# Decode attention on one core: the rows of the two output stores laid out for eight DMA engines instead of sixteen

## The chip, the core and the metric

The kernel runs on one core of one Trainium2 chip. The metric is the device time of the program in microseconds (us). The kernel before the change took 184.66 us, the median of three runs (184.62 to 184.82).

A core has the engines TensorE (PE; its weight loads are PEld), VectorE (DVE), ScalarE (ACT), GpSimd (POOL) and SyncE (SP). SP does not compute here: it issues DMAs and waits. ScalarE issues some DMAs too. Either queue's DMAs are carried out by the core's 16 DMA engines. SBUF is the on-chip memory of 128 partitions, PSUM is where TensorE writes its sums.

## The reference

One step of decoding with a sliding window: 32 sequences, one query token each, 32 query heads over 8 key/value heads, a window of 512 positions of a cache of 2048, heads of 128 elements, bf16.

```python
W = min(4096, max(256, Sk // 4))                     # 512
q = (x @ wq).reshape(B, Sq, Hq, Dh)                  # 32 x 32 heads x 128
k = jnp.repeat(k_cache[:, :, Sk - W:, :], rep, axis=1)
v = jnp.repeat(v_cache[:, :, Sk - W:, :], rep, axis=1)
scores = jnp.einsum("bhqd,bhkd->bhqk", q, k) * (Dh ** -0.5)
p = softmax(scores, axis=-1)
o = jnp.einsum("bhqk,bhkd->bhqd", p, v)
return o.reshape(B, Sq, Hq * Dh) @ wo                # 32 x 1 x 512
```

## The kernel before

**Tiles and rounds.** The 32 sequences are worked on in eight rounds q of four sequences. For a round, one 4 MB load brings the keys (K_sb, two buffers) and one or two loads the values (V_sb, two buffers), with the 128 partitions holding 4 sequences x 8 heads x 4 quarters of the window. The orders of the work on TensorE, VectorE and ScalarE are written out by hand in three lists (PE_OPS, DVE_OPS, ACT_OPS, lines 19 to 33), SP's order of loads in a fourth (LOADS, line 35). Each entry is a letter and a round; semaphores between them come from the function `needs`.

**One round.** VectorE transposes the keys (T, line 499). TensorE makes the scores (S), VectorE their maxima (M), ScalarE the exponentials (X), VectorE divides by the sums (N). TensorE moves the probabilities to the partitions of the values (E), ScalarE gathers them (G), VectorE and ScalarE spread them with a mask (B), and TensorE multiplies with the values (P, line 391). VectorE and ScalarE copy the result out of PSUM (C), and TensorE folds it so that the 128 elements of a head lie where the last product needs them: the fold F (line 403) for 120 of the 128 elements, the fold H (line 412) for the other eight.

**The columns of the sums.** The result of F stands in PSUM and ScalarE copies it to `o_sel` (op D, `folded`, line 569); H's result goes to `o_ext` (op U, `folded_ext`, line 574). `o_sel` is 128 partitions x 30 x 32 columns and `o_ext` 64 x 8 x 32; the last index is the sequence. Round q writes the four neighbouring columns 4q to 4q+3.

**The last product.** When the last round's D and U are done, TensorE multiplies with wo (lines 429 and 443): the 32 columns of `o_sel[:, i, :]` are the weights, so column m becomes row m of the result. The four strips c of the output's 512 columns go to four groups of 32 partitions of `Y_ps`, with n = 2 (c % 2) + c // 2 as the strip of wo. wo itself comes in three pieces (line 275), issued after the last values. At the end VectorE copies partitions 0 to 63 of `Y_ps` to `out_sb[:, 0]` (line 532) and ScalarE partitions 64 to 127 to `out_sb[:, 1]` (line 590). So partition 32c+m of `out_sb`, for c of 0 and 1, holds half c of the output row of column m, 256 elements of bf16 or 512 bytes.

**The stores.** The function `store` (line 236) waits for both copies and issues one DMA for a half: SP stores half 0 as its last work, ScalarE half 1. Each takes 32 partitions to 32 rows of the output, 16 KB. Both add to the one semaphore `sem_out`, and after the end of the block SP waits for 32 there, 16 for each DMA (line 594). With that the program ends.

Of the kernel before, what the change touches and what calls it, by code (L numbers as in the profile page):

```python
# [48 lines left out]
def bass_standalone__sliding_block_cached__sampling_kernel(  # L49
# [45 lines left out]
    def needs(op):  # L95
        kind, q = op[0], op[1]
        spread = lambda q: [("B", q, h) for h in range(HKV)]
        picks = lambda q: [("C", q, r) for r in range(4)]
        d = []
        if kind == "T":  # L100
            d = [("S", q - 1, op[2])]
        elif kind == "S":
            d = [("T", q, op[2]), ("X", q - 1)]
        elif kind == "M":
            d = [("S", q, 1)]
        elif kind == "X":
            d = [("M", q), ("N", q - 1)]
        elif kind == "N":
            d = [("X", q), ("E", q - 1)]
        elif kind == "E":  # L110
            d = [("N", q), ("G", q - 1)] + [("U", p) for p in before(op, "H")]
        elif kind == "G":
            d = [("E", q)] + spread(q - NG)
        elif kind == "B":
            d = [("G", q), ("P", q - 2, 31)]
        elif kind == "P":
            d = spread(q) + picks(q - 1)
        elif kind == "C":
            d = [("P", q, 31), ("F", q - 2), ("H", q - 2)]
        elif kind == "F":  # L120
            d = picks(q) + ([("D", q - 1)] if q < NQ - 1 else [])
        elif kind == "D":
            d = [("F", q)]
        elif kind == "H":
            d = picks(q) + [("U", q - 1)] + [("G", p) for p in before(op, "E")]
        elif kind == "U":
            d = [("H", q)]
        return [ends[n] for n in d if n[1] >= 0]

    with ExitStack() as es:  # L130
# [15 lines left out]
        o_sel = sb("o_sel", [P, NI, B], BF16)  # L146
        o_ext = sb("o_ext", [64, NX, B], BF16)
# [28 lines left out]
        ps = es.enter_context(nc.psum_tensor("ps", [P, 8, 512], F32))  # L176
        S_ps, EP_ps, O_ps, F_ps, Y_ps = ps[:, 0], ps[:, 1], ps[:, 2:6], ps[:, 6], ps[:, 7]

        def folds(q):
            return (F_ps if q < NQ - 1 else S_ps)[:, 0:4 * NI]  # L180

# [11 lines left out]
        s = {n: sem(n) for n in names}  # L193
# [42 lines left out]
        def store(eng, c):  # L236
            eng.wait_ge(s["out_y"], 2)
            eng.dma_start(
                out.rearrange("b s (c n) -> c (b s) n", c=2)[c],
                out_sb[32 * c:32 * c + 32, :, :].rearrange("b e n -> b (e n)"),  # L240
            ).then_inc(sem_out, 16)

        @block.sync
        def _(sp):
            wait = Waits(sp)
            load_wq(1)
            wo_h = wo.rearrange("(h r) n -> h (r n)", r=DH)
            wo_r = wo_h[:, 0:4 * NI * D].rearrange("h (d m) -> h d m", d=4)
            for op in ops_of(" ".join(LOADS)):
                kind, q = op[0], op[1]  # L250
                if kind == "K":
                    if q >= 2:
                        wait([ends["T", q - 2, 1]])
                    sp.dma_start(K_sb[q % 2][:, :], rows(k_cache, q)).then_inc(sem_k[q % 2], 16)  # L254
                elif kind == "V":
                    if q == 1:
                        sp.wait_ge(s["pe_q"], 8)
                    r0, r1 = (4 * g for g in V_PIECES[q][op[2]:op[2] + 2])
                    if q >= 2:
                        wait([ends["P", q - 2, r1 // 4 - 1]])  # L260
                    sp.dma_start(  # L261
                        V_sb[q % 2][:, r0 * DH:r1 * DH], rows(v_cache, q, r0, r1)
                    ).then_inc(sem_v[q % 2][op[2]], 16)
                elif kind == "A":
                    wait([ends["Z", 0]])
                    h0, h1, k, p0 = HEADS[q]
                    n = (h1 - h0) // k
                    sp.dma_start(  # L268
                        wx_row[p0:p0 + 4 * n:1 if k == 4 else 4, :],
                        wo_h[h0:h1, 4 * NI * D:].rearrange("(k j) m -> j k m", k=k),  # L270
                    ).then_inc(sem_wx, 16)
                else:
                    wait([ends["T", NQ - 2, 1]])
                    i0, i1 = WOP[q]
                    sp.dma_start(  # L275
                        wo_sb[:, i0:i1, :].rearrange("p i n -> p (i n)"),
                        wo_r[:, :, i0 * D:i1 * D],
                    ).then_inc(sem_wo[q], 16)
            store(sp, 0)

        @block.gpsimd
# [43 lines left out]
        def _(pe):  # L325
# [73 lines left out]
            def fold(q):  # L399
                if q == 0:  # L400
                    pe.wait_ge(s["dve_c"], 7 + len(HEADS))
                for d in range(4):
                    ins = pe.matmul(  # L403
                        folds(q),
                        lhsT=F_sb[:, d].rearrange("p h d -> p (h d)"),
                        rhs=C_sb[:, q % 2, :, NI * d:NI * d + NI],
                        start=d == 0, stop=d == 3, tile_position=(0, 0),
                    )
                return ins
# [40 lines left out]
        def spread_args(q, h):  # L450
            return bd[:, q % 2, :, h, :], PTc[:, q % NG], mask[:, h:h + 1]

        def pick_args(q, r):
            pr = slice(32 * r, 32 * r + 32)
            return C_sb[pr, q % 2], O_ps[pr, :, r * DH:(r + 1) * DH]
# [78 lines left out]
        @block.scalar  # L534
        def _(act):
            wait = Waits(act)
            act.wait_ge(s["pool_j"], 1)
            act.activation(junk[:, 1:2], junk[:, 0:1], ACTF.Exp).then_inc(s["act_warm"], 1)
            for n in range(4):
                act.wait_ge(s["pe_q"], 2 * n + 2)  # L540
                act.activation(  # L541
                    Q_row[:, 1024 * n + 512:1024 * n + 1024], ps[:, 2 * n + 1], ACTF.Copy
                ).then_inc(s["act_q"], 1)
            act.wait_ge(s["dve_c"], 3)

            def exponential(q):
                return act.activation(  # L547
                    P_f32[:, :].rearrange("p (k r) -> p k r", k=KB),
                    S_ps.rearrange("p (r k) -> p k r", k=KB), ACTF.Exp,
                    bias=negmax[:, q:q + 1], scale=SCALE, accum_out=sums[:, q:q + 1],  # L550
                )

            def gather(q):
                return act.activation(  # L554
                    PTc[:, q % NG], EP_ps.rearrange("p (e r) -> p r e", e=REP), ACTF.Copy)

            def spread(q, h0, h1):
                for h in range(h0, h1):
                    o, i, m = spread_args(q, h)
                    ins = act.activation(o, i, ACTF.Copy, scale=m)  # L560
                return ins

            def pick(q, r0, r1):
                for r in range(r0, r1):
                    ins = act.activation(*pick_args(q, r), ACTF.Copy)  # L565
                return ins

            def folded(q):
                return act.activation(
                    o_sel[:, :, 4 * q:4 * q + 4],  # L570
                    folds(q).rearrange("p (b i) -> p i b", b=4), ACTF.Copy)

            def folded_ext(q):
                return act.activation(
                    o_ext[:, :, 4 * q:4 * q + 4],
                    EP_ps[0:64, 0:4 * NX].rearrange("p (b i) -> p i b", b=4), ACTF.Copy)

            def zero(_):
                act.wait_ge(s["pool_qbd"], 4 * NQ)
                return act.activation(  # L580
                    wx_row, junk[0:64, 0:1].to_broadcast([64, NX * D]), ACTF.Copy
                )

            run = {"X": exponential, "G": gather, "B": spread, "C": pick, "D": folded,
                   "U": folded_ext, "Z": zero}
            for op in orders["ACT"]:
                wait(needs(op))
                run[op[0]](*op[1:]).then_inc(op_sem["ACT", op[0]], 1)
            act.wait_ge(s["pe_Y"], 2)
            act.activation(out_sb[:, 1, :], Y_ps[64:128, 0:P], ACTF.Copy).then_inc(s["out_y"], 1)  # L590
            store(act, 1)

        regions.close()
# [29 lines left out]
```

## Time and profile before

| what | value |
|---|---|
| median of three runs | 184.66 us (184.62 to 184.82) |
| the profiled execution's own time | 184.67 us |
| its span, first to last instruction | 183.3 us |
| mean granted TensorE clock | 0.814 |
| TensorE busy | 121.8 us (66%) |
| VectorE busy | 106.6 us (58%) |
| ScalarE busy | 54.0 us (29%) |
| HBM read | 75.53 MB, 412 GB/s over the span |
| SP's DMA queue (q1) | 3553 packets, 75.52 MB |
| ScalarE's DMA queue (q10) | 112 packets, 0.05 MB |
| ScalarE copies to o_sel (line 569), eight | 271 ns median |
| ScalarE copies to o_ext (line 574), eight | 184 ns median |
| issue of the store, SP / ScalarE | 0.37 / 0.39 us, both begin at 181.56 us |
| store, from issue to landing, SP / ScalarE | 1.5 / 1.7 us |
| SP's last wait, for the stores | 0.9 us |

A line of the page's groups names the line of the program, the engine, the operation, the tiles as out<-in, the shape and the count; behind the bar stand the busy time, the mean of one instruction, and the idle time before these instructions with what ended it. The lower-case q behind an engine's name (SPq, ACTq) means its sequencer, which issues DMAs and waits. A busy share says little by itself: the stages have different limits, and the chain of waits tells which one sets the end.

### The profile page before, as it was taken

What the parts mean: (1) busy time and instruction counts of PE and PEld (TensorE: products, weight loads), DVE (VectorE), ACT (ScalarE), POOL (GpSimd) and SP (SyncE); (2) the same over time, 40 slices, a digit from 0 to 9 for tenths busy, and PEclk for the clock granted to TensorE, in tenths of its full rate; (3) what the DMA queues carried; (4) which work ended last, traced back from release to release, by engine and by line L of the source; (5) the groups of instructions that cost most, each with busy time, mean ns of one, the idle gap of its engine ahead of it and who ended that gap; (6) DMA issues with size and microseconds to landing.
All of it is one profiled execution on the core that took longest, in us unless ns stands there. A gap on an engine that the chain in (4) does not pass through costs nothing.

```text
span 183.3 us, 3872 instructions
## 1 busy us (share of the span) xinstructions
PE 121.8 (66%) x1676; PEld 59.3 (32%) x1676; DVE 106.6 (58%) x109; ACT 54.0 (29%) x101; POOL 17.1 (9%) x53
## 2 busy tenths in 40 slices
PE   0089204426798795449945995340799978999994
PEld 0034000011653452313521352000254533655573
DVE  0041999796469731973289326999825994703030
ACT  3000300010863357101651135001053693703040
POOL 7900050200100100002000200001000000000000
PEclk9999965555589999756995599655559999999999
DMA  6998999999998999999999999999999999999992
GB/s 226 411 501 358 458 458 447 393 415 458 458 426 372 458 454 426 401 429 458 427 415 415 452 427 418 415 451 451 415 415 411 433 418 433 422 435 408 429 380 72
DMA packets 3681, 75.80 MB, mean 414 GB/s; under 512 B 465, under 2 KB 561, under 8 KB 689
## 3 DMA queue, kind: packets, MB, share of 16 engines
q1 hardware_dynamic: 3553, 75.52, 96.6%
q8 instruction: 13, 0.21, 0.5%
q10 hardware_dynamic: 112, 0.05, 0.1%
q14 instruction: 3, 0.02, 0.0%
HBM read 75.53 MB, written 0.03 MB: 412 GB/s over the span
## 4 chain that ended last, share of the span: by engine, by line
DMA 76%; DVE 13%; SPq 4%; PE 3%; issue 3%; ACT 0%; DVEq 0%
DMA K_sb<-in_k_cache_dram 50%; DMA V_sb<-in_v_cache_dram 16%; DVE KT_sb L499 12%; DMA K_sb<-in_wo_dram 10%; PE ps L391 2%; SPq L268 2%; SPq L254 1%; SPq L261 1%; PE ps L429 1%; PE ps L361 1%; SPq L210 0%; DVE C_sb L524 0%; SPq L275 0%; DVE maxv L505 0%; ACT P_bf L590 0%
## 5 line engine op out<-in xcount | busy, mean ns | idle before, releaser
L499 DVE STREAM_TRANSPOSE KT_sb<-K_sb 128x4096 f32<-128x4096 f32 x16 | 70.6, 4434 | 11.2 <-DMA K_sb<-in_k_cache_dram 11.0
L391 PE MATMUL ps<-V_sb,bd 32*128 32x512 bf16 x1024 | 62.9, 397 | 3.8 <-DMA V_sb<-in_v_cache_dram 2.2
L361 PE MATMUL ps<-KT_sb,QBD 128*32 128x512 bf16 x256 | 26.1, 546 | 37.5 <-DVE KT_sb L499 26.9
L391 PEld LDWEIGHTS ps<-V_sb,bd 32*128 32x128 bf16 x1024 | 27.8, 97 | 36.2 <-issue 12.2
L361 PEld LDWEIGHTS ps<-KT_sb,QBD 128*32 128x32 bf16 x256 | 6.7, 115 | 53.8 <-DVE KT_sb L499 33.2
L547 ACT ACTIVATE P_f<-ps,negmax 128x512 f32<-128x512 f32 x8 | 5.5, 687 | 60.5 <-DVE negmax L507 60.5
L560 ACT ACTIVATE bd<-PTc,mask 128x512 bf16<-128x512 bf16 x31 | 20.1, 711 | 0.3
L565 ACT ACTIVATE C_sb<-ps 32x512 f32<-32x512 f32 x22 | 12.9, 588 | 23.4 <-PE ps L391 23.2
L318 POOL COPY QBD<-QT_sb 32x128 bf16<-32x128 bf16 x32 | 9.3, 289 | 106.4 <-PE ps L361 89.8
L519 DVE TENSOR_SCALAR bd<-PTc,mask 128x512 bf16<-128x512 bf16 x33 | 9.4, 349 | 14.0 <-ACT PTc L554 14.0
L524 DVE COPY C_sb<-ps 32x512 f32<-32x512 f32 x10 | 6.9, 693 | 13.9 <-PE ps L391 13.8
L403 PE MATMUL ps<-C_sb,F_sb 128*128 128x120 f32 x64 | 9.4, 291 | 6.8 <-ACT C_sb L565 6.5
L376 PE MATMUL ps<-P_bf,E_sb 128*128 128x128 bf16 x128 | 11.0, 254 | 0.8 <-DVE P_bf L513 0.8
L403 PEld LDWEIGHTS ps<-C_sb,F_sb 128*128 128x128 f32 x64 | 8.0, 195 | 9.6 <-ACT C_sb L565 8.3
L505 DVE TENSOR_REDUCE maxv<-ps 128x1 f32<-128x512 f32 x8 | 5.5, 687 | 9.4 <-PE ps L361 9.3
L376 PEld LDWEIGHTS ps<-P_bf,E_sb 128*128 128x128 bf16 x128 | 9.3, 115 | 4.9 <-DVE P_bf L513 2.8
L554 ACT ACTIVATE PTc<-ps 128x512 bf16<-128x512 f32 x8 | 4.8, 594 | 18.3 <-PE ps L376 18.2
L343 PE MATMUL ps<-V_sb,bd 128*128 128x512 bf16 x32 | 8.7, 441 | 0.8 <-DVE bd L461 0.8
L331 PE MATMUL ps<-bd 32*128 32x128 bf16 x4 | 0.6, 295 | 9.2 <-DMA bd<-in_x_dram 9.2
L461 DVE CAST bd<-ps 128x512 bf16<-128x512 f32 x1 | 0.7, 692 | 9.8 <-PE ps L331 9.8
L541 ACT ACTIVATE KT_sb<-ps 128x512 bf16<-128x512 f32 x4 | 2.1, 602 | 14.2 <-PE ps L343 14.2
L488 DVE CAST KT_sb<-ps 128x512 bf16<-128x512 f32 x4 | 2.5, 684 | 5.9 <-PE ps L343 5.9
(37 smaller groups left out, 43.9 us busy)
## 6 DMA issues: line engine op xcount, KB each, us to landing
K_sb<-in_k_cache_dram SPq DMA_DIRECT2D x8, 4096.0 KB, 25.2
V_sb<-in_v_cache_dram SPq DMA_DIRECT2D x5, 4096.0 KB, 29.6
V_sb<-in_v_cache_dram SPq DMA_DIRECT2D x4, 2048.0 KB, 20.6
V_sb<-in_wq_dram SPq DMA_DIRECT2D x2, 2048.0 KB, 9.8
K_sb<-in_wo_dram SPq DMA_DIRECT2D x1, 2560.0 KB, 17.2
V_sb<-in_v_cache_dram SPq DMA_DIRECT2D x1, 2304.0 KB, 14.2
V_sb<-in_v_cache_dram SPq DMA_DIRECT2D x1, 1792.0 KB, 14.8
K_sb<-in_wo_dram SPq DMA_DIRECT2D x1, 1024.0 KB, 19.1
```

Of the source, the lines that this page charges most:

```text
L318: pool.tensor_copy(QBD[pr, q % 2].rearrange("p (w t) (h c) -> p w t h c", w=2, h=HKV)[:, :, :, :, 4 * b:4 * b + 4], QT_sb[pr, q].rearrange ...
L343: ins = pe.matmul(ps[:, n], lhsT=xT_sb[:, kt, :], rhs=wq_sb[:, kt, n * 512:(n + 1) * 512], start=kt == 0, stop=kt == DKT - 1, tile_positio ...
L361: ins = pe.matmul(S_ps[32 * c:32 * c + 32, :], lhsT=QBD[:, q % 2, 2 * w + t, c0:c0 + 32], rhs=KT_sb[:, w, :, KB * h:KB * h + KB, t], start ...
L376: ins = pe.matmul(EP_ps[:, e * R:(e + 1) * R], lhsT=E_sb[:, k, e].rearrange("p m j -> p (m j)"), rhs=P_bf[:, k * R:(k + 1) * R], start=k = ...
L391: ins = pe.matmul(O_ps[:, b, :], lhsT=bd[pr, q % 2, 4 * g:4 * g + 4].rearrange("p r h e -> p (r h e)"), rhs=V_sb[q % 2][pr, 512 * g:512 * ...
L403: ins = pe.matmul(folds(q), lhsT=F_sb[:, d].rearrange("p h d -> p (h d)"), rhs=C_sb[:, q % 2, :, NI * d:NI * d + NI], start=d == 0, stop=d ...
L499: return dve.transpose(KT_sb[:, w].bitcast(F32).rearrange("p r c t -> p r (c t)"), K_sb[q % 2][:, :].bitcast(F32).rearrange("p (r w c) -> ...
L505: dve.tensor_reduce(maxv[:, q:q + 1], S_ps, AX.X, ALU.max).then_inc(s["dve_m"], 1)
L519: ins = dve.tensor_scalar(o, i, m, None, op0=ALU.mult)
L524: ins = dve.tensor_copy(*pick_args(q, r))
L560: ins = act.activation(o, i, ACTF.Copy, scale=m)
L565: ins = act.activation(*pick_args(q, r), ACTF.Copy)
```

## The change

The 32 columns of `o_sel` and `o_ext` are filled in another order, and the stores undo it. Round q holds the sequences 4q+i, i from 0 to 3. Before, sequence 4q+i had column 4q+i. After, with the sequence written as 8a+j (a from 0 to 3, j from 0 to 7), it has column 4j+a. For round q that is a = q // 2 and j = 4 (q % 2) + i, so the round writes the columns 16 (q % 2) + q // 2 + 4i: four columns with a step of four. Row m = 4j+a of the last product then belongs to sequence 8a+j, and the store's target is written as eight groups j of four rows a of 256 elements, in place of 32 rows of 256 elements. The source, 32 partitions of 512 bytes, stays as it is.

```diff
+        def columns(q):
+            first = 16 * (q % 2) + q // 2
+            return slice(first, first + 13, 4)
...
         def store(eng, c):
             eng.wait_ge(s["out_y"], 2)
             eng.dma_start(
-                out.rearrange("b s (c n) -> c (b s) n", c=2)[c],
+                out.rearrange("(a j) s (c n) -> c j (a s) n", a=4, c=2)[c],
                 out_sb[32 * c:32 * c + 32, :, :].rearrange("b e n -> b (e n)"),
             ).then_inc(sem_out, 16)
...
             def folded(q):
                 return act.activation(
-                    o_sel[:, :, 4 * q:4 * q + 4],
+                    o_sel[:, :, columns(q)],
                     folds(q).rearrange("p (b i) -> p i b", b=4), ACTF.Copy)
 
             def folded_ext(q):
                 return act.activation(
-                    o_ext[:, :, 4 * q:4 * q + 4],
+                    o_ext[:, :, columns(q)],
                     EP_ps[0:64, 0:4 * NX].rearrange("p (b i) -> p i b", b=4), ACTF.Copy)
```

The instructions on each engine and their number stay the same, and so does the number of DMAs.

## The prediction

> **What bounds the kernel now.** I read the chain of work that ended last, then the timeline of its end, then the groups that the diff touches, then the DMA queues and issues. The head of the chain:
>
> ```profile
> DMA 76%; DVE 13%; SPq 4%; PE 3%; issue 3%; ACT 0%; DVEq 0%
> ```
>
> Three quarters of the span are loads, and ScalarE, whose copies the diff re-addresses, has no share of the chain. The timeline of the end, from the last fold on:
>
> ```profile
> 177.65 0.27 ACT L569 ACTIVATE o_sel<-ps 128x120 bf16<-128x120 f32 x1 [1.15 <-PE ps L403]
> 177.88 0.19 ACT L574 ACTIVATE o_ext<-ps 64x32 bf16<-64x32 f32 x1
> 177.97 1.13 PEld L429 LDWEIGHTS ps<-K_sb,o_sel 128*32 128x32 bf16 x80 [0.24 <-ACT o_sel L569]
> ...
> 180.24 0.93 PE L429 MATMUL ps<-K_sb,o_sel 128*32 128x128 bf16 x40 [0.41 <-DMA K_sb<-in_wo_dram]
> ...
> 181.26 0.27 ACT L590 ACTIVATE P_bf<-ps 64x128 bf16<-64x128 f32 x1 [3.19 <-PE ps L429]
> 181.56 0.37 SPq L238 DMA_DIRECT2D out_dram<-P_bf  x1
> 181.56 0.39 ACTq L238 DMA_DIRECT2D out_dram<-P_bf  x1
> ```
>
> Columns: start, length in us, then the instruction, in brackets the idle time before it. TensorE, given the last o_sel at 177.9, stands idle 0.41 us for a piece of wo before 180.24: so much may o_sel come later at no cost. From 181.56 only the two stores are left, and SP's last wait is for them. The waits of SP, then the landing of the stores in the DMA view, then the stretch of the stores (length, five engines, clock, DMA share, GB/s):
>
> ```profile
> SPq L594 <- DMA out_dram<-P_bf: 0.9, 1, 0.9
> ```
>
> ```profile
> out_dram<-P_bf SPq DMA_DIRECT2D x1, 16.0 KB, 1.5
> out_dram<-P_bf ACTq DMA_DIRECT2D x1, 16.0 KB, 1.7
> ```
>
> ```profile
> 182.40:182.60 0.20, 0.00 (x0) 0.00 (x0) 0.00 (x0) 0.00 (x0) 0.00 (x0) 1.00 0.55 128
> 182.60:182.80 0.20, 0.00 (x0) 0.00 (x0) 0.00 (x0) 0.00 (x0) 0.00 (x0) 1.00 0.16 36
> 182.80:183.26 0.46, 0.00 (x0) 0.00 (x0) 0.00 (x0) 0.00 (x0) 0.00 (x0) 1.00 0.00 0
> ```
>
> The bytes move between 182.4 and 182.75; in the last 0.46 us nothing moves and SP still waits. The trace's single records of DMA packets and semaphore updates, which no view prints, divide the tail: issues until 181.932 (SP) and 181.956 (ACT); first packet of SP's store at 182.424, of ACT's at 182.509; 64 row packets of 512 B, most 27 to 40 ns, and 32 completion packets, 16 for each store, the last ending at 182.726; then 32 updates of the output's semaphore from 182.801 to 183.233, the first gap 31 ns and each of the other thirty 13 or 14 ns. The first update follows the first completion packet (182.479) by 0.32 us, the last follows the last (182.717) by 0.52. So the updates queue, for some 0.2 us, one in 13.3 ns. SP's wait ends at 183.249, the span at 183.27.
>
> The profiled execution took 184.67 us: the span and 1.40 us around it. The sum is made against 184.67; the median of the three runs is 184.66.
>
> **The change part by part.**
>
> *The ScalarE copies into o_sel and o_ext* (eight of each): same instructions, same elements, only that four columns lie 8 bytes apart. Rows: 271 and 184 ns, of 120 and 32 elements, so about 1 ns an element. No ScalarE row writes single bf16 elements; the near ones write runs of four or whole rows. Bounds: nothing, and a doubling of the part that goes by the element, +0.12 and +0.03 us. Even then the last pair delays TensorE by 0.15 us of the 0.41 it idles; the seven earlier pairs stand in an engine busy 29% and off the chain. I take 0. If the wo load landed 0.41 us earlier, the 0.15 would show.
>
> *TensorE* reads all 32 columns as before; only the order of the result's rows differs. 0. *The two result copies, 0.28 and 0.27 us*, are unchanged. 0.
>
> *Issue, engines.* Each store goes from 16 engines with two rows to 8 with four. The four loads of x on ScalarE's queue differ in this: 2, 6, 10 and 14 rows, as many completion packets. The timeline has
>
> ```profile
> 1.34 0.27 ACTq L204 DMA_DIRECT2D bd<-in_x_dram  x1
> ...
> 1.64 0.31 ACTq L204 DMA_DIRECT2D bd<-in_x_dram  x1
> ...
> 1.98 0.35 ACTq L204 DMA_DIRECT2D bd<-in_x_dram  x1
> ```
>
> for 6, 10 and 14 engines (271, 314, 351 ns): 10 ns an engine, and on to 371 ns for 16, where the stores have 373 and 392. Eight fewer engines: -0.08 us. Their semaphore got 36 updates where 2+6+10+14 is 32, so each DMA on fewer than 16 engines adds one for the missing count; these issues hold that cost.
>
> *Issue, dimensions.* The target becomes three-dimensional (8 by 4 by 256) against a source of 32 by 256. The K loads have such a shape against wq's plain rows:
>
> ```profile
> 0.74 0.42 SPq L210 DMA_DIRECT2D V_sb<-in_wq_dram  x1
> ...
> 43.49 0.54 SPq L254 DMA_DIRECT2D K_sb<-in_k_cache_dram  x1
> ```
>
> 0.54-0.42: +0.12 us. The two nearest in shape are loads of wo's remainder on five engines, 20 rows in groups of four (0.90 us) and five plain rows (0.73): +0.17. I take +0.12, since K's issue follows a wait on an idle queue, as the store's does. Ends: 0, and a whole issue as long as the 0.90. With the engines: 0.37-0.08+0.12 = 0.41, +0.04 us on each queue, the two side by side.
>
> *Issue to first packet.* 0.49 us with 16 engines (SP), 0.39 with two (x: issue ended at 1.302, packet at 1.695): 7 ns an engine at most, -0.06 for eight; ScalarE's 0.55 against 0.39 would be -0.09. I take 0, as one store's packets already waited on the other's, and keep -0.09.
>
> *Packets.* Both stores may land on the same eight engines: eight rows an engine instead of four. SP's first rows start over about 0.17 us from engine to engine (some 11 ns each), so the eighth starts at about 182.51; eight rows at 30 ns and two completions of 9 ns bring its end to 182.77, against 182.726: +0.04. Ends: -0.05 (ACT's store on other engines) and +0.30 (the stage of 0.30 us doubles). For the engines' choice, the Trainium skill (DMA: Bandwidth & Descriptors, Why a DMA increments its semaphore by 16 and not by 1) states that such a DMA takes the lowest-numbered ones and that the issuing sequencer writes the missing count at once; the 36 updates agree with the latter, and no view tells engines apart.
>
> *Updates.* 16 from engines instead of 32. Served one in 13.3 ns, 16 take 0.2 us; the first completion now comes after four rows (about 182.54), its update at 182.86, the sixteenth at 183.08 (one gap of 31, fourteen of 13.3). The last completion packet starts at 182.76 and its update is due 0.32 later, also 183.08 to 183.09. Against 183.233: -0.14 us, packets included. Ends: 0, if the gaps are those of rows being written, of which there are as many; -0.21, sixteen gaps saved whole.
>
> Sum: +0.04 (issue) +0 -0.14 (packets and updates) = -0.10 us: 184.57.
>
> **The rivals.**
>
> *The updates wait for rows, not for each other.* 64 rows in 0.43 us is 6.7 ns a row; the queue would then be as long as now. For: the rows of all engines go to one 32 KB region. Against: rows of many engines mix irregularly, and thirty equal gaps speak for a server of updates. Time: 184.67+0.04+0 = 184.71. The same skill page (Anatomy of one DMA, of GpSimd's path) lays most of a store's fixed time to the receipt from the target memory, which would give the same 184.71; the two completions of the x loads, with SBUF as target, were followed 0.34 us later by their updates, no less than the 0.32 here, so the trace does not bear it out.
>
> *Every per-engine cost halves and the shape costs nothing.* Issue -0.08, first packet -0.09, updates -0.21, packets 0: 184.29, just on the bound of a fall, and a little more if ScalarE's issue, now 392, falls with SP's to 0.29 (-0.10): 184.27. For: the rows of x carry all slopes. Against: K's dimension, the eight rows an engine.
>
> *Half the engines, double the transfer.* The skill page's section Rules for kernel authors says to keep a size that is a multiple of 16 outermost, so that all 16 engines are used. By rows: the packet stage of 0.30 us doubles and hides the shorter queue of updates: 184.67+0.30 = 184.97. Against: the starts are staggered and cover most.
>
> *The issue takes the long form, on the other side.* The nearest shape (20 rows, groups of four, five engines) took
>
> ```profile
> 157.37 0.90 SPq L268 DMA_DIRECT2D QT_sb<-in_wo_dram  x1
> ```
>
> Both stores at 0.90 instead of 0.37: +0.53, less the 0.14: 185.06. It makes the kernel slower by over 0.2% from an issue of 0.88 us on. Against: it stood in a row of issues beside running loads, and the plain issues behind it (0.73 to 0.63) were long too, with five and two engines.
>
> **How the numbers follow.** The forecast, 184.57, has 0.38 with its neighbours between 184.45 and 184.70; rows as the limit, 184.71, 0.13; all per-engine costs halved, about 184.27, 0.27; the doubled transfer, 184.97, 0.07; the long issue, 185.06 and more, 0.15. 0.2% is 0.37 us, about what a measurement of this kernel can tell from no change. Of the 0.27 I put 0.20 beyond 184.29: faster 0.20. Slower 0.15. The rest, 0.65, within. The range goes from 184.20 to 185.07: it leaves out some 0.05 below and half of the long issue above.
>
> **What would show it.** The issues of the stores at about 0.41 us instead of 0.37 and 0.39 (0.29: the shape is free; 0.90: the long form). The packets of ScalarE's queue fall from 112 to 104, of 32 completions 16 remaining. The updates: 16 of the engines and two single ones ahead, gaps of 13 ns (27 would say rows). Landing 1.6 at most for the later store instead of 1.7; SP's last wait shorter by about 0.1. The o_sel and o_ext copies at 271 and 184 ns. Wrong it would be, above all, if the loads before 180.9 took another time, which nothing in the change touches, or if the issue costs more than 0.9 us.

## The result and the profile after

The changed kernel takes 185.22 us (median of nine runs, 184.94 to 185.40) against 184.73 us for the kernel before beside it (nine runs, 184.62 to 184.96): slower by 0.28%, ratio 1.0028 with a 95% interval of 1.0020 to 1.0037. That is 0.49 us, and the time lies 0.15 us above the stated range.

The profiled execution of the changed kernel is its shortest run, 184.94 us, with a span of 183.62 us; its loads happened to end a little earlier, and the stores began at 181.44 us instead of 181.56. So spans are not compared here, but the tail from the first store's issue on: 1.71 us before, 2.18 us after, +0.48 us, close to the 0.49 us between the medians.

The timeline of the end of the changed kernel (start, length, instruction; lines of the program are four further on):

```profile
177.60 0.42 ACT L573 ACTIVATE o_sel<-ps 128x120 bf16<-128x120 f32 x1 [1.01 <-PE ps L407]
177.83 0.25 ACT L578 ACTIVATE o_ext<-ps 64x32 bf16<-64x32 f32 x1
178.07 1.12 PEld L433 LDWEIGHTS ps<-K_sb,o_sel 128*32 128x32 bf16 x80 [0.39 <-ACT o_sel L573]
...
180.13 0.92 PE L433 MATMUL ps<-K_sb,o_sel 128*32 128x128 bf16 x40 [0.20 <-DMA K_sb<-in_wo_dram]
...
181.14 0.27 ACT L594 ACTIVATE P_bf<-ps 64x128 bf16<-64x128 f32 x1 [3.06 <-PE ps L433]
181.44 0.78 SPq L242 DMA_DIRECT2D out_dram<-P_bf  x1
181.44 0.77 ACTq L242 DMA_DIRECT2D out_dram<-P_bf  x1
```

The issue of each store has doubled, 0.78 and 0.77 us instead of 0.37 and 0.39. The copy to o_sel takes 0.42 us instead of 0.27, and TensorE's idle time before the last piece of wo shrinks from 0.41 to 0.20 us (0.15 of that is the copy; the piece of wo also came a little earlier): the copy is slower, but still covered. The same tail in stretches (length, five engines, clock, DMA share, GB/s):

```profile
181.40:182.85 1.45, 0.00 (x0) 0.00 (x0) 0.00 (x0) 0.01 (x1) 0.00 (x0) 1.00 0.00 0
182.85:183.00 0.15, 0.00 (x0) 0.00 (x0) 0.00 (x0) 0.00 (x0) 0.00 (x0) 1.00 0.54 157
183.00:183.15 0.15, 0.00 (x0) 0.00 (x0) 0.00 (x0) 0.00 (x0) 0.00 (x0) 1.00 0.24 62
183.15:183.62 0.47, 0.00 (x0) 0.00 (x0) 0.00 (x0) 0.00 (x0) 0.00 (x0) 1.00 0.00 0
```

The first packet comes at 182.85, 1.41 us after the issue began; before, that took 0.87 us. Between first and last packet little has changed. The DMA queues and SP's waits say that the rows did go as intended:

```profile
q10 hardware_dynamic: 104, 0.05, 0.1%
```

```profile
SPq L598 <- DMA out_dram<-P_bf: 0.6, 1, 0.6
```

104 packets on ScalarE's queue instead of 112: eight completion packets fewer, so eight engines. SP's last wait became shorter, 0.6 us instead of 0.9, because it began later, and not because the stores landed sooner: a wait that shrinks is no gain by itself. Only half of that delay is the longer issue. Between the issue and the wait SP and ScalarE each have a DRAIN instruction at the end of their part of the block, which the timeline does not list; it too became longer (least, median and greatest length in ns), first before, then after:

```profile
L593 ACTq DRAIN  x1: 146/146/146, 182.0 to 182.0; - x1
L593 SPq DRAIN  x1: 116/116/116, 182.0 to 182.0; - x1
```

```profile
L597 ACTq DRAIN  x1: 492/492/492, 182.3 to 182.3; - x1
L597 SPq DRAIN  x1: 562/562/562, 182.3 to 182.3; - x1
```

Measured from the start of the issue, SP's wait begins 0.80 us later: 0.40 by the issue and 0.45 by SP's DRAIN, less some smaller gaps. So the issuing engines are held for some time after the issue has ended; whether the store's first packet waits for the same thing is not shown.

The single records of packets and semaphore updates divide the tail. "Issue" runs from the first issue's start to the later one's end, "to packet" on to the first packet, "packets" to the end of the last completion packet, "updates" to the last update of the output's semaphore, "end" to the end of the span. The other columns belong to the experiments below.

| us | before | after | e16x2 | inner | rows8 | one_plain | one_8x4 | packed |
|---|---|---|---|---|---|---|---|---|
| issue | 0.40 | 0.78 | 0.65 | 0.70 | 0.34 | 0.37 | 0.78 | 0.37 |
| to packet | 0.47 | 0.64 | 0.64 | 0.65 | 0.46 | 0.49 | 0.64 | 0.49 |
| packets | 0.30 | 0.27 | 0.49 | 0.50 | 0.18 | 0.23 | 0.17 | 0.30 |
| updates | 0.51 | 0.47 | 0.38 | 0.37 | 0.49 | 0.36 | 0.36 | 0.36 |
| end | 0.03 | 0.03 | 0.03 | 0.03 | 0.03 | 0.03 | 0.03 | 0.03 |
| sum | 1.71 | 2.18 | 2.20 | 2.24 | 1.50 | 1.49 | 1.97 | 1.56 |

So the loss of 0.48 us is +0.38 us of issue and +0.17 us between issue and first packet; packets and updates give back 0.04 us each.

### The profile page after: what moved, and what is told of

The parts are those of the page before. It is cut to its first block, busy times and chain, and to the rows that moved or that the text cites. A ratio compares the mean times of both kernels' runs of the same rounds, so it can differ in the third digit from the quotient of the medians.

```text
span 183.6 us, 3872 instructions
## 1 busy us (share of the span) xinstructions
PE 121.4 (66%) x1676; PEld 60.1 (33%) x1676; DVE 106.7 (58%) x109; ACT 54.7 (30%) x101; POOL 17.1 (9%) x53
## 4 chain that ended last, share of the span: by engine, by line
DMA 76%; DVE 13%; SPq 4%; PE 3%; issue 3%; ACT 0%; DVEq 0%
DMA K_sb<-in_k_cache_dram 49%; DMA V_sb<-in_v_cache_dram 16%; DVE KT_sb L503 12%; DMA K_sb<-in_wo_dram 10%; PE ps L395 2%; SPq L272 2%; SPq L258 1%; SPq L265 1%; PE ps L433 1%; PE ps L365 1%; SPq L214 0%; DVE C_sb L528 0%; SPq L279 0%; DVE maxv L509 0%; ACT P_bf L594 0%
## 5 line engine op out<-in xcount | busy, mean ns | idle before, releaser
L395 PE MATMUL ps<-V_sb,bd 32*128 32x512 bf16 x1024 | 63.8, 401 | 4.7 <-DMA V_sb<-in_v_cache_dram 2.3
L365 PE MATMUL ps<-KT_sb,QBD 128*32 128x512 bf16 x256 | 24.9, 525 | 36.8 <-DVE KT_sb L503 26.0
L395 PEld LDWEIGHTS ps<-V_sb,bd 32*128 32x128 bf16 x1024 | 28.3, 98 | 37.2 <-issue 13.6
L407 PE MATMUL ps<-C_sb,F_sb 128*128 128x120 f32 x64 | 10.6, 317 | 6.8 <-ACT C_sb L569 6.5
L407 PEld LDWEIGHTS ps<-C_sb,F_sb 128*128 128x128 f32 x64 | 9.0, 218 | 9.6 <-ACT C_sb L569 8.3
L380 PE MATMUL ps<-P_bf,E_sb 128*128 128x128 bf16 x128 | 10.2, 242 | 0.8 <-DVE P_bf L517 0.8
L380 PEld LDWEIGHTS ps<-P_bf,E_sb 128*128 128x128 bf16 x128 | 8.6, 109 | 4.9 <-DVE P_bf L517 2.8
```

The costliest lines, as they stand in the source:

```text
L365: ins = pe.matmul(S_ps[32 * c:32 * c + 32, :], lhsT=QBD[:, q % 2, 2 * w + t, c0:c0 + 32], rhs=KT_sb[:, w, :, KB * h:KB * h + KB, t], start ...
L380: ins = pe.matmul(EP_ps[:, e * R:(e + 1) * R], lhsT=E_sb[:, k, e].rearrange("p m j -> p (m j)"), rhs=P_bf[:, k * R:(k + 1) * R], start=k = ...
L395: ins = pe.matmul(O_ps[:, b, :], lhsT=bd[pr, q % 2, 4 * g:4 * g + 4].rearrange("p r h e -> p (r h e)"), rhs=V_sb[q % 2][pr, 512 * g:512 * ...
L407: ins = pe.matmul(folds(q), lhsT=F_sb[:, d].rearrange("p h d -> p (h d)"), rhs=C_sb[:, q % 2, :, NI * d:NI * d + NI], start=d == 0, stop=d ...
```

## The experiments

Which property of the new store makes its issue long: the third dimension of the target (theory S), or that it runs on fewer than 16 engines and so adds the missing count to the semaphore (theory E)? And do the slower copies of ScalarE take part (theory C)? The first four runs tell these apart.

**The third dimension with all 16 engines (e16x2).**

```diff
         def columns(q):
-            first = 16 * (q % 2) + q // 2
-            return slice(first, first + 13, 4)
+            first = 8 * (q % 4) + q // 4
+            return slice(first, first + 7, 2)
...
-                out.rearrange("(a j) s (c n) -> c j (a s) n", a=4, c=2)[c],
+                out.rearrange("(a j) s (c n) -> c j (a s) n", a=2, c=2)[c],
```

> The target keeps a third dimension (16 groups of 2 rows) but all 16 engines, as many rows an engine as before. Theory S (the third dimension is what makes the issue long): the stores' issues take 0.75 to 0.90 us and the kernel is as slow as the changed one, 185.1 to 185.4 us, ratio about 1.003. Theory E (fewer than 16 engines, with the extra update for the missing count, is what makes it long): issues at 0.37 to 0.50 us, 32 updates, ratio 0.999 to 1.001.

185.15 us, ratio 1.0020 (1.0011 to 1.0030). The timeline of its stores:

```profile
181.64 0.65 SPq L242 DMA_DIRECT2D out_dram<-P_bf  x1
181.65 0.64 ACTq L242 DMA_DIRECT2D out_dram<-P_bf  x1
```

With 16 engines, two rows each and 32 updates as in the kernel before, issue and gap are nearly as long as in the changed kernel, against theory E. The issue is 0.10 us below the bottom of what theory S expected, and the tail is as long in the end for another reason: the packets of the second queue begin 0.27 us after those of the first, against 0.09 us in the kernel before and 0.10 in the changed one.

**Eight engines without a third dimension (rows8).**

```diff
-                out.rearrange("b s (c n) -> c (b s) n", c=2)[c],
-                out_sb[32 * c:32 * c + 32, :, :].rearrange("b e n -> b (e n)"),
+                out.rearrange("b s (c n) -> c (b s) n", c=2)[c, 0:8],
+                out_sb[32 * c:32 * c + 8, :, :].rearrange("b e n -> b (e n)"),
```

> Columns as before; each store takes only its first 8 rows, plain (8 by 256), so 8 engines without a third dimension; the other 24 rows of each half are left out and never written. Theory S: issues at 0.28 to 0.32 us (the slope of the x loads), ScalarE's queue with 80 packets (8 rows and 8 completions less 24 and 8), first packet 0.45 to 0.49 us after the issue. Theory E: issues at 0.65 us or more. The span after the issue gets shorter in either case, since 48 of 64 rows are gone.

The timeline of its stores, and its queue of ScalarE:

```profile
181.74 0.34 SPq L238 DMA_DIRECT2D out_dram<-P_bf  x1
181.75 0.31 ACTq L238 DMA_DIRECT2D out_dram<-P_bf  x1
```

```profile
q10 hardware_dynamic: 80, 0.04, 0.1%
```

The run took 184.65 us, with 48 of the 64 rows left out. Eight engines and the extra update cost nothing at the issue of a plain store: 0.34 and 0.31 us (SP's a little above what theory S named), less than 16 plain engines with four times the rows take (0.37 and 0.39), and the first packet follows after 0.46 us. Theory E is out. Together with e16x2 this lays the loss on the form with the third dimension. One thing fits neither theory: with only 16 updates, the last one still came 0.49 us after its packet.

**The columns alone (cols_only).** The changed kernel with the store of the kernel before.

```diff
-                out.rearrange("(a j) s (c n) -> c j (a s) n", a=4, c=2)[c],
+                out.rearrange("b s (c n) -> c (b s) n", c=2)[c],
```

> Only the order of the columns changes; the stores are the plain ones, so the output's rows lie in another order than the reference's. The copies to o_sel take 0.42 us and those to o_ext 0.25 to 0.31, as in the changed kernel. Theory S and theory E alike: they are hidden behind the load of wo, ratio 0.9995 to 1.0005 (184.65 to 184.85 us). A rival theory C (the copies cause a good part of the loss): ratio 1.001 or more.

184.72 us, ratio 0.9999 (0.9989 to 1.0008). Its copies, with least, median and greatest length in ns:

```profile
L573 ACT ACTIVATE o_sel<-ps x8: 419/424/452, 63.0 to 177.7; 128x120 bf16<-128x120 f32 x8
L578 ACT ACTIVATE o_ext<-ps x8: 233/293/331, 63.2 to 177.9; 64x32 bf16<-64x32 f32 x8
```

The copies are as slow as in the changed kernel and cost nothing. Theory C is out.

**The store alone (store_only).** The kernel before with the store of the changed one.

```diff
-                out.rearrange("b s (c n) -> c (b s) n", c=2)[c],
+                out.rearrange("(a j) s (c n) -> c j (a s) n", a=4, c=2)[c],
```

> Only the stores change; the columns stay in order, so the output's rows lie in another order than the reference's. Theories S and E: the whole loss, ratio 1.002 to 1.0035, issues at 0.77 us, the end 2.18 us after the stores' issue begins (1.71 before). Theory C: ratio under 1.002.

185.25 us, ratio 1.0026 (1.0016 to 1.0035), the copies back at 271 and 184 ns, and

```profile
181.69 0.78 SPq L238 DMA_DIRECT2D out_dram<-P_bf  x1
181.69 0.77 ACTq L238 DMA_DIRECT2D out_dram<-P_bf  x1
```

The tail from the issue on is 2.17 us. The new target of the store alone carries the loss.

**One store instead of two (one_plain, one_8x4).** The next question was why 16 updates instead of 32 gained so little, and whether the two long issues hold each other up. In both runs

```diff
-            store(act, 1)
...
-        nc.sync.wait_ge(sem_out, 32)
+        nc.sync.wait_ge(sem_out, 16)
```

once in the kernel before, once in the changed one. Both leave half 1 of the output unwritten.

> Only SP's store of half 0 is left, plain; ScalarE's store of half 1 is left out and SP waits for 16. Theory Q (the updates are served one in 13.3 ns, whoever sends them): 16 updates; completions start over about 0.17 us, so hardly a queue: the last update 0.33 to 0.37 us after its completion packet instead of 0.52, the end about 0.25 us earlier after the issue (1.71 to 1.45). Theory O (a second store on the same engine has its update held until the first store's is through): also a short lag here, since there is no second store, 0.32 to 0.36, but with gaps that are those of the completions, about 11 ns, and not 13.3. Theory R (each update waits for rows to be written, 6.7 ns a row): 32 rows, the same short lag.

> Only SP's store of half 0 is left, in the form of 8 groups of 4 rows; ScalarE's is left out and SP waits for 16. Theory S (third dimension): the issue stays at 0.77 us though nothing is issued beside it; a rival (two issues of this form hold each other up): under 0.60 us. First packet: 0.64 us after the issue's end if the form sets it, under 0.50 if the other store does. Theory O: the eight updates come 0.33 to 0.36 after their completions, the last one too (0.47 with two stores).

The runs took 184.28 and 184.94 us. The timeline of the plain store, then that of the store in groups:

```profile
181.48 0.37 SPq L238 DMA_DIRECT2D out_dram<-P_bf  x1
```

```profile
181.63 0.78 SPq L242 DMA_DIRECT2D out_dram<-P_bf  x1
```

Issue (0.78) and gap (0.64) are the same with nothing beside the store: both belong to the form, as theory S has it. On the updates: in the plain run the 16 completions start over 0.163 us, but their updates stretch over 0.210 us, the last eleven gaps again 13 or 14 ns; in the other run eight completions start over 0.065 us and their updates stretch over 0.093, seven gaps of 13.3. So the updates do queue (theory Q; theory O had expected the gaps of the completions). But with one store the last update follows its completion's end by 0.36 us in both forms, whether 16 updates queue or eight. The lags near 0.5 us appear only where there are two stores, and there only where the second queue's completions come within 0.1 us of the first's: in e16x2, inner and e4x8, where they come 0.19 to 0.26 us later, the lag is 0.34 to 0.38.

**Four groups of eight (e4x8).**

```diff
         def columns(q):
-            first = 16 * (q % 2) + q // 2
-            return slice(first, first + 13, 4)
+            return slice(q, q + 25, 8)
...
-                out.rearrange("(a j) s (c n) -> c j (a s) n", a=4, c=2)[c],
+                out.rearrange("(a j) s (c n) -> c j (a s) n", a=8, c=2)[c],
```

> 4 groups of 8 rows, so 4 engines. The issue was 0.65 us with 16 groups of 2 and 0.77 with 8 of 4. Theory S1 (the issue goes up with the rows in a group, by some 0.06 us a row): about 1.0 us, the kernel at 185.4 to 185.7 us. Theory S2 (a fixed price of the third dimension and 10 ns an engine): below 0.77. The o_sel copies, with a step of 16 bytes, at 0.42 us or more.

185.16 us in one run. Stores and copies of ScalarE:

```profile
181.62 0.72 SPq L241 DMA_DIRECT2D out_dram<-P_bf  x1
181.63 0.72 ACTq L241 DMA_DIRECT2D out_dram<-P_bf  x1
```

```profile
L572 ACT ACTIVATE o_sel<-ps x8: 699/704/718, 62.3 to 177.8; 128x120 bf16<-128x120 f32 x8
L577 ACT ACTIVATE o_ext<-ps x8: 502/630/660, 62.5 to 178.0; 64x32 bf16<-64x32 f32 x8
```

0.72 us is below 0.77, so the price doesn't grow with the rows of a group (S1 falls). S2 fits these two, at 13 ns an engine, but not the 0.65 of 16 groups of two, where it would give 0.88. The issue in this form takes between 0.65 and 0.78 us, and no simple rule for it came out. The runs on 16 engines, e16x2 and inner (next), have the two lowest values, so within this form a share for fewer engines is not excluded.

**A third dimension inside the rows (inner).** Must the groups cut through the rows, or does any third dimension cost?

```diff
-                out.rearrange("b s (c n) -> c (b s) n", c=2)[c],
-                out_sb[32 * c:32 * c + 32, :, :].rearrange("b e n -> b (e n)"),
+                out.rearrange("b s (e c n) -> c (b s) e n", e=2, c=2)[c],
+                out_sb[32 * c:32 * c + 32, :, :],
...
-                            n = 2 * (c % 2) + c // 2
+                            n = c
```

The last edit stands in both loops of the last product.

> The strips of wo are taken in plain order, so each row of a half of the output comes as two runs of 128 elements that lie 256 apart: the target has three dimensions (32 by 2 by 128), but its outer one is still the 32 rows, all 16 engines are used, and the columns are as before. Theory S1 (any third dimension in the target makes the issue long): 0.60 to 0.80 us, first packet 0.63 to 0.65 after it, ratio 1.002 or more. Theory S2 (only where the outer dimension of the target is another than that of the source, 8 or 16 against 32): 0.37 to 0.45 us, first packet 0.47 to 0.50, ratio 0.999 to 1.001, with 64 instead of 32 row packets for each store.

185.22 us, ratio 1.0021 (1.0011 to 1.0030):

```profile
181.69 0.69 SPq L238 DMA_DIRECT2D out_dram<-P_bf  x1
181.69 0.69 ACTq L238 DMA_DIRECT2D out_dram<-P_bf  x1
```

The numbers are those of S1: all 16 engines run, and still the issue takes 0.69 us and the first packet 0.65 more. So the groups need not cut through the rows. But the run does not decide between S1 and S2 as they were meant, because the pattern is not the intended one. The runs of 128 elements follow each other through the output at one even step of 256, so in the built program the target is 64 rows of 128 elements, two dimensions, and it is the source that has three, 32 partitions with two runs each. The outer dimensions are then 64 and 32 and differ, as S2 requires for a long issue. What the run does show is that a third dimension in the target is not needed: one on the source side goes with the same price. Rows of 256 bytes are not the reason, since the plain stores of two_plain (below) have them too and begin with issues of 0.37 and 0.39 us. Part of the tail of inner is its own: it has twice as many row packets, and its second queue too begins 0.27 us after the first.

**The same form twice (two_8x4, two_plain).** Is it the first use of the form on a queue that is slow? Each store is cut into two of 128 columns, first in the changed kernel, then, plain, in the kernel before.

```diff
-            eng.dma_start(
-                out.rearrange("(a j) s (c n) -> c j (a s) n", a=4, c=2)[c],
-                out_sb[32 * c:32 * c + 32, :, :].rearrange("b e n -> b (e n)"),
-            ).then_inc(sem_out, 16)
+            for e in range(2):
+                eng.dma_start(
+                    out.rearrange("(a j) s (c e n) -> c e j (a s) n", a=4, c=2, e=2)[c, e],
+                    out_sb[32 * c:32 * c + 32, e, :],
+                ).then_inc(sem_out, 16)
...
-        nc.sync.wait_ge(sem_out, 32)
+        nc.sync.wait_ge(sem_out, 64)
```

> The changed kernel with each store cut in two along the columns (128 elements, 256-byte rows), so that each queue issues the form of 8 groups of 4 rows twice in a row. Theory S (the price belongs to the form): the second issue takes 0.70 to 0.85 us like the first. A rival W (the first use of the form on a queue is slow, as the first of the x loads was with 0.55 against 0.27): the second issue takes under 0.55 us.

> The kernel before with each store cut in two along the columns (128 elements, 256-byte rows), plain. Beside the run with 8 groups of 4: first issues at 0.37 to 0.40 us, second ones at 0.35 to 0.45. The span is longer than before by the second issue less what it hides.

The issues of the groups, first and second of each queue:

```profile
181.58 0.78 SPq L243 DMA_DIRECT2D out_dram<-P_bf  x1
181.58 0.77 ACTq L243 DMA_DIRECT2D out_dram<-P_bf  x1
```

```profile
182.39 0.68 ACTq L243 DMA_DIRECT2D out_dram<-P_bf  x1
182.40 0.74 SPq L243 DMA_DIRECT2D out_dram<-P_bf  x1
```

and the second ones of the plain form:

```profile
181.94 0.41 SPq L239 DMA_DIRECT2D out_dram<-P_bf  x1
181.94 0.44 ACTq L239 DMA_DIRECT2D out_dram<-P_bf  x1
```

The second use costs 0.68 to 0.74 us against 0.41 to 0.44 plain (ScalarE's 0.68 a little under what theory S named): the price belongs to the form, rival W is out. The runs took 185.96 and 184.97 us. Four plain stores, two more than needed, have a tail of 2.15 us from the first issue on, no longer than the 2.18 us of two in groups. The 64 updates of the plain run came in two rows of 32, from 182.732 to 183.152 and from 183.212 to 183.625, 13 or 14 ns apart but for the first gap: the clearest look at their rate.

**One plain store of whole rows (packed).** The runs with one store pointed to a kernel with one issue and 16 updates that leaves nothing out: the four strips side by side in 32 partitions.

```diff
+        def strip(c):
+            n = 2 * (c % 2) + c // 2
+            return out_sb[:, n * P:(n + 1) * P], Y_ps[32 * c:32 * c + 32, 0:P]
...
-            dve.wait_ge(s["pe_Y"], 1)
-            dve.tensor_copy(out_sb[:, 0, :], Y_ps[0:64, 0:P]).then_inc(s["out_y"], 1)
+            for c in (0, 2):
+                dve.wait_ge(s["pe_Y"], c + 1)
+                dve.tensor_copy(*strip(c)).then_inc(s["out_y"], 1)
...
-            act.wait_ge(s["pe_Y"], 2)
-            act.activation(out_sb[:, 1, :], Y_ps[64:128, 0:P], ACTF.Copy).then_inc(s["out_y"], 1)
-            store(act, 1)
+            for c in (1, 3):
+                act.wait_ge(s["pe_Y"], c + 1)
+                act.activation(*strip(c), ACTF.Copy).then_inc(s["out_y"], 1)
```

TensorE signals each strip as it is summed, SP's store waits for four copies and takes 32 plain rows of 1024 bytes, and the end waits for 16 updates.

> Columns as before. The four strips of the result are copied side by side into 32 partitions of 1024 bytes, two copies on VectorE and two on ScalarE, each as soon as its strip is summed, and SP alone stores 32 rows of 1024 bytes, plain, on 16 engines: 16 updates instead of 32, one issue. Issue 0.37 to 0.38 us, first packet 0.47 to 0.49 after it, packets 0.25 to 0.30, last update 0.33 to 0.40 after the last completion (0.52 before): the end 0.1 to 0.25 us earlier after the issue. The copies: the last begins at the same time as before and takes about as long (0.27), so the issue begins within 0.1 us of before. Together 184.50 to 184.75 us, ratio 0.9985 to 1.0000.

184.91 us, ratio 1.0004 (0.9995 to 1.0014): no difference. The timeline shows both halves of the answer:

```profile
180.49 0.91 PE L432 MATMUL ps<-K_sb,o_sel 128*32 128x128 bf16 x40 [0.41 <-DMA K_sb<-in_wo_dram]
...
181.42 0.59 DVE L536 CAST P_bf<-ps 32x128 bf16<-32x128 f32 x2 [4.82 <-PE ps L432]
181.46 0.56 ACT L595 ACTIVATE P_bf<-ps 32x128 bf16<-32x128 f32 x2 [3.13 <-PE ps L432]
182.05 0.37 SPq L238 DMA_DIRECT2D out_dram<-P_bf  x1
```

The tail from the issue on did become shorter, 1.56 instead of 1.71 us. But the four strips are summed at nearly the same time, so two copies follow each other on each engine, 0.59 us on VectorE from first start to last end instead of 0.28. From the start of TensorE's work on the last piece of wo to the issue it takes 1.56 us instead of 1.32, 0.24 more, and the tail saves 0.15. My expectation that the last copy would begin at the same time was wrong.

**What was not tested: a mark in the program.** In the program that is built from these kernels, a DMA instruction can carry a mark, `ant_dge_precooked`. All plain stores have it, and so have the loads of x and wq. No store of the long form has it, nor have the loads of K, V and wo. So in the stores the third dimension and the missing mark always go together. The kernel before has loads that part them. Of the loads of wo's remainder, the second to fourth have two dimensions (5, 5 and 2 plain rows) and no mark; the load of wo itself behind them (line 275) has three dimensions and no mark:

```profile
158.32 0.73 SPq L268 DMA_DIRECT2D QT_sb<-in_wo_dram  x1
```

```profile
159.09 0.67 SPq L268 DMA_DIRECT2D QT_sb<-in_wo_dram  x1
```

```profile
159.81 0.63 SPq L268 DMA_DIRECT2D QT_sb<-in_wo_dram  x1
```

```profile
160.49 0.61 SPq L275 DMA_DIRECT2D K_sb<-in_wo_dram  x1
```

The plain ones are no quicker to issue than the three-dimensional one. In the whole kernel before, every load without the mark was issued in 0.53 us or more, and every DMA with it in 0.42 or less, but for the first load of x (0.55). This speaks for the mark, and not the number of dimensions, as what goes with a long issue. It is argued only: these are loads, issued beside running transfers, and a plain store without the mark was not run. For this kernel the outcome is the same either way, since the stores lost the mark with the change. What the mark does was not measured.

## Why the prediction was wrong

It forecast no measurable difference, and the kernel became slower by 0.28%. By its steps:

- **What bounds the kernel, and where the change acts:** right. Nothing before the stores mattered, and the store alone gives the whole loss (1.0026).
- **The copies:** right in effect (0.9999), wrong in size. Bounded at +0.12 and +0.03 us, they took +0.15 and +0.11 (medians of cols_only). The bound of twice the part that goes by the element was too narrow; the cover of 0.41 us was larger.
- **Issue, engines:** -0.08 us was the order of it. Plain on eight engines, rows8 showed 0.34 and 0.31 against 0.37 and 0.39, so -0.04 and -0.08; it also has 8 rows instead of 32, so the share of the engines alone is not shown.
- **Issue, dimensions: the step that failed.** I took +0.12 us from the loads of K and set aside the row of the nearest shape, the load in groups on five engines at 0.90 us, because of its neighbours. Its difference from the plain load behind it, the 0.17 that the prediction also named, would have been too small as well, since that load is itself long. Against rows8, the form costs 0.44 (SP) and 0.46 us (ScalarE), and against the plain stores of 32 rows 0.40 and 0.38; the issue is 0.78 us where the prediction had 0.41.
- **Issue to first packet: failed too.** I took 0 and kept only an end below nothing; no row showed a loss, and I gave none. Every store of the long form had 0.64 or 0.65 us (the table; also store_only and e4x8), the plain ones 0.46 to 0.49: +0.17 us.
- **Packets:** +0.04 forecast, -0.04 measured; inside the ends.
- **Updates:** they do queue at 13.3 ns, and the step's saving on them was mis-sized. Packets and updates together were to give 0.14 us and gave 0.07. The updates of the first queue's eight completions began 0.34 us after them as reckoned, but those of the second queue, whose completions came 0.10 us later, began 0.19 us after the first queue's, at 183.477 and not at 183.390.

The sum: +0.38 +0.17 -0.04 -0.04 = +0.47 us (0.48 before rounding) against the forecast of -0.10.

Of the rivals, the long issue was the one that came true, with the sign and the place. Its time, 185.06, was too low: the issue cost 0.38 more and not 0.53, but the 0.17 before the first packet was missing and the updates gave too little. The rival of halved costs was contradicted by the form's price. Rows as the limit of the updates is not excluded by the rate alone where rows are two to an update; but in one_8x4 eight updates of four rows each came 13.3 ns apart, where 6.7 ns a row would have needed 27. The doubled transfer did not occur: the packet stage was no longer.

By the Trainium skill (DMA: Bandwidth & Descriptors, Rules for kernel authors), keeping a multiple of 16 outermost would have avoided eight engines; e16x2 and inner keep it and lose 0.20 and 0.21% all the same, so that rule is not what decides here.

**What stays open.** Why the issue of the form takes 0.65 to 0.78 us, in an order that follows neither the engines nor the rows; whether it is the third dimension, unequal outer dimensions of source and target, or the missing mark; and what holds back the second queue's updates. That completions of two stores on one engine need some 0.19 us between their updates would fit the changed kernel (0.193 us between the two queues' first updates, completions 0.10 apart), store_only (0.194) and rows8 (0.185, completions 0.04 apart), where it would explain the late last update. In e4x8 the completions are themselves 0.19 us apart, so it tests nothing. In the changed kernel each of the second queue's eight completions comes 0.100 us after one of the first's, in the same pattern, which speaks for the same eight engines; but no record tells the engines apart, so it is only argued.

## What to carry to other kernels

A small store that ends a kernel is all latency: price the issue and the time to the first packet by the shape of its access pattern first, and the engines and bytes last. Here a plain store got from the start of the issue to the first packet in 0.87 us with 16 engines (0.80 with eight, of fewer rows), and one with a third dimension in 1.3 to 1.4, with 4, 8 or 16 engines. And where a trace has one row of nearly the shape that a change introduces, its price belongs in the forecast even if its surroundings look unusual; a step for which no row exists needs an end on the side of loss too.

## What the runs showed of the hardware that was not expected

- ScalarE's copy of 128x120 elements to bf16 took 271 ns with four neighbouring elements in a run, 304 with a step of 4 bytes, 424 with 8 and 704 with 16 (medians of the kernel before, e16x2, cols_only and e4x8); the small one of 64x32 went from 184 over 196 and 293 to 630 ns. It is hidden here, but a step in the output of a ScalarE copy is not free.
- The output's semaphore took no more than one update of a store's completion in 13.3 ns; with four plain stores (two_plain) 32 came in a row at that rate, twice.
- Between the first packets of the two queues lay 0.09 us with plain stores, 0.10 with 8 groups of 4, 0.22 with 4 groups of 8, and 0.27 with 16 groups of 2 or 64 half rows, although both issues ended within 0.02 us of each other. In two_8x4, with half rows and a second issue behind the first, it was 0.27 with 8 groups of 4 too. In e16x2 and inner the DRAIN of the later queue also ends 0.27 us after the other's, so the delay arises before the packets; in e4x8 the two end 0.08 us apart.
